# A written order on every engine, q transposed by DMA and merged products in an attention and long-convolution kernel

## The chip, the cores and the metric

The kernel runs on one core of a Trainium2 chip. A core has TensorE (PE in the profile; it loads weights, PEld, and multiplies into PSUM), VectorE (DVE), ScalarE (ACT), GpSimd (POOL) and SyncE (SP), each with its own queue of instructions, and 16 DMA engines that all queues share. SBUF and PSUM have 128 partitions. The metric is the device time of one execution in microseconds (us).

## The reference

Linear attention with an RMS norm feeds a gated long convolution. B = 8 batches, H = 8 heads, S = 576 times, D = 64; d_model is 512.

```python
kv = np.einsum('bhsd,bhse->bhde', k, v)
out = np.einsum('bhsd,bhde->bhse', q, kv)
rms = np.sqrt(np.mean(out * out, axis=-1, keepdims=True) + 1e-06)
x = (out / rms * g_norm)            # then heads side by side: (B, S, 512)

proj = x @ w_proj                   # 512 -> 1536
x1, x2, x3 = proj[..., :D], proj[..., D:2*D], proj[..., 2*D:]   # D = 512 here
X2 = np.fft.rfft(x2, n=S, axis=1)
H = np.fft.rfft(filter_fft, n=S, axis=0)[None, :, :]
x2_conv = np.fft.irfft(X2 * H, n=S, axis=1)
y = (x1 * x2_conv * x3) @ w_out
```

Inputs and output are float32 in DRAM; the kernel computes in bfloat16 with float32 sums.

## The kernel before

**Tiling.** One batch after the other, features on the partitions (four blocks of 128 features, two heads each) until the Fourier stage, frequencies on the partitions there. The Fourier transforms are matmuls with cosine and sine tables (IV, FW, FX), made once at the start (L167 to L210). Symmetries cut them down: time is split into thirds and halves, the sums and differences of these (fold, L291) are what is projected.

**The steps of one batch.** kv (L214) multiplies k and v over time, in four chunks of 128 times and a tail of 64, and evicts the two halves of each head pair into kvblk, a block-diagonal matrix of 128 x 128 per pair. qtr (L236) transposes q with 36 matmuls against an identity and evicts them to qT. att_o (L258) multiplies qT by kvblk, two full matmuls for a feature block, and evicts twice: the square (ACT) and the value times g_norm. att_r (L273) sums the squares of a head by a matmul with the 0/1 matrix ind and evicts the inverse root; att_x multiplies. fold forms rr (192 columns) and ab (384 columns). proj2 (L363) projects both for x2: full blocks of 128 rows, and 64-row rests in matmuls of 64 columns each (L372, L384). fft (L388) has three parts: g = 1 (L404 to L406), g = 0 (L399 to L401), g = 2 (L414 to L416). Each result in PSUM is multiplied twice on DVE with the filter's spectrum HH (L408, L409); the two products are added on POOL (L411) or, for g = 0 of later batches, on DVE (L412). proj13 (L419) makes x1 and x3 (the gates) in 16 matmuls per feature block and multiplies them. inv (L436) is the inverse transform: odd and even parts, one copied by ACT, sum and difference on DVE, three operations of a recombination w, and fin, the product with the gates, giving yg. outp (L484) multiplies yg by w_out in chunks of 128 rows, two chunks per PSUM tile, and stores 64 rows by 2 per DMA on SP's queue; the last 64 rows of two batches share one tile (L492).

**What sets the order.** The text is a loop over batches in which batch b's Fourier and gate steps are interleaved with batch b + 1's attention. The framework's scheduler orders instructions within that; only some are pinned with keep_in_program_order. PSUM is one pool of four tiles of two banks, given out in turn. Loads go through POOL's queue, two batches ahead, k and v each in a main and a tail DMA, q in two halves (L66 to L82); row stores through SP's queue. At the start, 33 matmuls on constant data (warm, L531) are placed on PE between the first steps. The filter is loaded twice, straight and reversed through an indirect DMA (L142, L147), and folded on DVE (L319); gen_h (L332) makes its spectrum.

Of the kernel before, what the change touches and what calls it, by code (L numbers as in the profile page):

```python
# [9 lines left out]
FP32 = mybir.dt.float32  # L10
# [5 lines left out]
P = 128  # L16
MAGIC = 3.0 * (2.0 ** 22)


@with_exitstack  # L20
def kernel(
# [11 lines left out]

# [8 lines left out]
    NSC = 5  # L46
    TAIL = S - 4 * P
    N1 = 97
    NM = 64

    nc.scalar.preload_act_table_set("trig_and_small")
    consts = ctx.enter_context(tc.tile_pool(name="consts", bufs=1))
    work = ctx.enter_context(tc.tile_pool(name="work", bufs=1))
    psp = ctx.enter_context(tc.tile_pool(name="psp", bufs=4, space=bass.MemoryType.PSUM))

    def ps_tile(name):
        return psp.tile([P, 2, 512], FP32, name=name, tag="ps")

    NR = S // 64
    kvm = [[consts.tile([P, H, 4, D], BF16, name="%sm%d" % (n, i)) for n in "kv"] for i in range(2)]
    kvt = [[consts.tile([P, H, D], BF16, name="%st%d" % (n, i)) for n in "kv"] for i in range(2)]
    qb = [consts.tile([P, 4, NR * D], BF16, name="qb%d" % i) for i in range(2)]

    def load_kv(b, *parts):
        for h0, h1 in parts:
            for i, src in enumerate((k, v)):
                nc.gpsimd.dma_start(  # L70
                    out=kvm[b % 2][i][:, h0:h1].rearrange("p h c d -> p h (c d)"),
                    in_=bass.AP(tensor=src.tensor, offset=src.offset + (b * H + h0) * S * D,
                                ap=[[4 * D, P], [S * D, h1 - h0], [1, 4 * D]]))
                if h0 == 0:
                    nc.gpsimd.dma_start(out=kvt[b % 2][i][:TAIL], in_=src[b, :, 4 * P:S, :].transpose([1, 0, 2]))

    def load_q(b):
        for g in range(2):
            nc.gpsimd.dma_start(  # L79
                out=qb[b % 2][64 * g:64 * g + 64].rearrange("p h (m x) -> p (h m) x", m=3),  # L80
                in_=bass.AP(tensor=q.tensor, offset=q.offset + (b * H + 4 * g) * S * D,
                            ap=[[3 * D, 64], [SB * D, 12], [1, 3 * D]]))  # L82


    kvblk = [consts.tile([P, 4, P], BF16, name="kvblk%d" % i) for i in range(2)]
    for i in range(2):
        for t in kvt[i]:
            nc.vector.memset(t[TAIL:P], 0.0)
        nc.vector.memset(kvblk[i], 0.0)
    bias_eps = consts.tile([P, 1], FP32)  # L90
    nc.vector.memset(bias_eps, 1e-6)

    W0 = math.pi / S
    cosb = consts.tile([P, 4], FP32)
    nc.vector.memset(cosb[:, 0:2], math.pi / 2)
    nc.vector.memset(cosb[64:P, 1:2], -math.pi / 2)
    nc.vector.memset(cosb[:, 2:4], -W0)
    nc.vector.memset(cosb[64:P, 3:4], W0)

    ind = consts.tile([P, P], BF16)  # L100
    nc.vector.memset(ind, 0.0)
    for h in range(2):
        nc.vector.memset(ind[64 * h:64 * h + 64, 64 * h:64 * h + 64], 1.0)  # L103

    load_q(0)

    kcol = consts.tile([P, 3], FP32)  # L110
    ki = consts.tile([P, 3], I32)
    nc.gpsimd.iota(ki[:, 0:1], pattern=[[0, 1]], base=0, channel_multiplier=3)
    nc.gpsimd.iota(ki[0:96, 1:2], pattern=[[0, 1]], base=1, channel_multiplier=3)
    nc.gpsimd.iota(ki[96:128, 1:2], pattern=[[0, 1]], base=2, channel_multiplier=3)
    nc.gpsimd.iota(ki[0:64, 2:3], pattern=[[0, 1]], base=2 + 3 * 32, channel_multiplier=3)
    nc.gpsimd.iota(ki[64:128, 2:3], pattern=[[0, 1]], base=2 + 3 * 32, channel_multiplier=3)
    tvi = work.tile([P, 2 * SB], I32, name="tvi", tag="yg", bufs=3)


    nc.gpsimd.iota(tvi, pattern=[[2 * SB, 2], [2, 3], [6, 64]], base=1, channel_multiplier=0)  # L120
    ident = consts.tile([P, P], BF16)
    make_identity(nc, ident)

    load_kv(0, (0, 4), (4, 8))
# [7 lines left out]
    for part in (1, 0, 2):  # L132
        load_w(wp[:, :, part * DM:(part + 1) * DM], moe_w_proj[:, part * DM:(part + 1) * DM])


    fa = work.tile([P, 3, DM], FP32, name="fa", tag="tpw", bufs=2)
    fc = work.tile([P, 3, DM], FP32, name="fc", tag="tpw", bufs=2)
    fidx = consts.tile([P, 3], I32)
    for a, r0, n, base in ((0, 0, 64, 0), (0, 64, 64, 1), (1, 0, 64, 2), (1, 64, 64, SB), (2, 0, 32, SB + 1)):
        nc.gpsimd.iota(fidx[r0:r0 + n, a:a + 1], pattern=[[0, 1]], base=S - 1 - base, channel_multiplier=-3)  # L140
    for r0, n, a, na, base, step in ((0, 64, 0, 2, 0, 2), (64, 64, 0, 2, 1, SB - 1), (0, 32, 2, 1, SB + 1, 1)):
        nc.gpsimd.dma_start(out=fa[r0:r0 + n, a:a + na], in_=bass.AP(  # L142
            tensor=moe_filter_fft.tensor, offset=moe_filter_fft.offset + base * DM,
            ap=[[3 * DM, n], [step * DM, na], [1, DM]]))
    for a in range(3):
        n = P if a < 2 else 32
        nc.gpsimd.indirect_dma_start(out=fc[:n, a], out_offset=None, in_=moe_filter_fft,  # L147
                                     in_offset=bass.IndirectOffsetOnAxis(ap=fidx[:n, a:a + 1], axis=0))

    load_q(1)  # L150
    load_kv(1, (0, 8))
    load_w(wo, moe_w_out)


# [489 lines left out]
```

## Time and profile before

| | |
|---|---|
| runs of the kernel | 240.43, 241.04, 243.11 us; median 241.04 |
| span of the profiled execution (first to last instruction) | 238.0 us |
| PE busy | 213.9 us, 90% |
| DVE busy | 197.2 us, 83% |
| ACT busy | 156.0 us, 66% |
| POOL busy | 72.1 us, 30% |
| mean granted TensorE clock | 0.993 |
| HBM read, written | 33.69 MB, 9.44 MB |

Busy shares are averages over a head that fills the pipeline, a middle of equal rounds and a tail that drains it, so they are to be read stage by stage. Matmul lengths include a pipeline delay and overlap; the distance from one start to the next is what a matmul costs. Idle time of an engine has the engine named that released it.

### The profile page before, as it was taken

The numbers are of one execution on the slowest core, as the hardware profiler recorded it, in microseconds if no ns is written. First come the engines' busy times: TensorE is split into PE (matmuls) and PEld (weight loads), VectorE is DVE, ScalarE is ACT, GpSimd is POOL, SyncE is SP. The second block draws the span as 40 slices with busy tenths as digits, with TensorE's granted clock in tenths as the row PEclk, the third lists the DMA queues.
The fourth block names the chain that finished last, engine by engine and source line by source line (L and its number), as shares of the span: only waits on it lengthen the run. The fifth ranks groups of instructions, "written<-read, shape, count | busy, mean of one in ns | idle before, by whom it ended". The sixth has DMA issues, their size and how long they took to land.

```text
span 238.0 us, 4900 instructions
## 1 busy us (share of the span) xinstructions
PE 213.9 (90%) x1960; PEld 128.5 (54%) x1960; DVE 197.2 (83%) x376; ACT 156.0 (66%) x237; POOL 72.1 (30%) x96
## 2 busy tenths in 40 slices
PE   4978897685999999999999999999999999999960
PEld 1434354363576657665667566656675666566420
DVE  7759574799989798979797989797979897999860
ACT  2754528971887689776977697769776977642520
POOL 7963971490280029000910091002100210021010
PEclk9999999999999999999999999999999999999997
DMA  6999999999099129914992399250033003400346
GB/s 63 163 190 230 227 192 197 191 192 108 3 155 198 45 77 158 203 38 126 121 193 74 91 118 188 83 135 0 4 88 88 3 0 91 132 0 3 94 122 181
DMA packets 45559, 27.17 MB, mean 114 GB/s; under 512 B 22274, under 2 KB 40706, under 8 KB 45538
## 3 DMA queue, kind: packets, MB, share of 16 engines
q0 software_dynamic: 40256, 17.70, 58.8%
q1 hardware_dynamic: 5122, 8.92, 13.9%
q8 instruction: 15, 0.25, 0.4%
q10 hardware_dynamic: 160, 0.26, 0.4%
q14 instruction: 6, 0.05, 0.1%
HBM read 33.69 MB, written 9.44 MB: 181 GB/s over the span
## 4 chain that ended last, share of the span: by engine, by line
PE 61%; ACT 15%; DVE 8%; DMA 8%; issue 3%; POOL 3%; POOLq 0%; DVEq 0%; ACTq 0%
PE ps_x L428 20%; PE ps_out L488 10%; ACT qT L256 6%; PE ps_x L378 6%; DMA fc<-in_moe_filter_fft_dram,fidx 5%; DMA km<-in_k_dram 3%; PE ps_x L384 2%; PE ps_x L369 2%; PE ps_o L265 2%; PE ps_r L280 2%; ACT kvblk L234 2%; PE ps_invo L454 2%; PE ps_inve L454 2%; PE ps_kv L223 2%; ACT osb L271 2%
## 5 line engine op out<-in xcount | busy, mean ns | idle before, releaser
L428 PE MATMUL ps_x<-x,wp 128*128 128x288 bf16 x512 | 68.0, 286 | 1.5 <-DVE FX L210 1.5
L428 PEld LDWEIGHTS <-wp 128*128 128x128 bf16 x512 | 49.8, 98 | 15.3 <-issue 2.6
L411 POOL TENSOR_TENSOR Y<-tpw 128x1024 bf16<-128x1024 f32 (+1 forms) x9 | 21.2, 2354 | 68.7 <-PE ps_x L428 43.2
L434 DVE TENSOR_TENSOR g<-ps_x,x 128x576 bf16<-128x576 f32 x32 | 24.1, 754 | 9.8 <-ACT x L432 9.7
L432 ACT CAST x<-ps_x 128x576 bf16<-128x576 f32 x32 | 20.7, 646 | 10.4 <-PE ps_x L428 10.4
L70 POOL DMA_DIRECT2D km<-in_k_dram x9 | 7.8, 871 | 64.4 <-PE ps_kv L223 64.4
L488 PE MATMUL ps_out<-wo,yg 128*128 128x512 bf16 x112 | 26.6, 379 | 0.0
L281 ACT ACTIVATE rstd<-ps_r,bias_eps 128x576 bf16<-128x576 f32 x32 | 23.3, 742 | 4.8 <-PE ps_r L280 4.8
L496 ACT COPY ot<-ps_out 128x1024 f32<-128x1024 f32 (+1 forms) x17 | 15.9, 937 | 13.8 <-PE ps_out L488 13.8
L266 ACT ACTIVATE sq<-ps_o 128x576 bf16<-128x576 f32 x32 | 20.7, 653 | 5.6 <-PE ps_o L265 5.6
L408 DVE TENSOR_TENSOR tpw<-ps_X,HH 128x1024 f32<-128x1024 f32 (+1 forms) x16 | 19.5, 1221 | 5.1 <-PE ps_X L406 4.4
L271 ACT ACTIVATE osb<-ps_o,g_col 128x576 bf16<-128x576 f32 x28 | 20.8, 742 | 0.0
L409 DVE TENSOR_TENSOR tpw<-ps_X,HH 128x1024 f32<-128x1024 f32 (+1 forms) x16 | 19.4, 1213 | 0.0
L458 ACT COPY os<-ps_invo 128x576 f32<-128x576 f32 x14 | 9.0, 640 | 12.9 <-PE ps_x L372 5.1
L488 PEld LDWEIGHTS <-yg 128*128 128x128 bf16 x112 | 10.8, 98 | 10.4
L265 PE MATMUL ps_o<-qT,kvblk 128*128 128x288 bf16 x64 | 12.8, 287 | 3.7 <-ACT kvblk L234 2.1
L378 PE MATMUL ps_x<-wp,ab 128*128 128x512 bf16 x64 | 15.5, 381 | 0.6 <-DVE ab L307 0.3
L256 ACT COPY qT<-ps_qT 128x1152 bf16<-128x1152 bf16 x14 | 15.1, 1122 | 0.1
L280 PE MATMUL ps_r<-sq,ind 128*128 128x288 bf16 x64 | 13.1, 286 | 1.6 <-ACT osb L271 0.8
L79 POOL DMA_DIRECT2D qb<-in_q_dram x16 | 12.5, 784 | 6.3 <-DMA wp<-in_moe_w_proj_dram 3.1
L535 PE MATMUL ps_w<-kvblk,ind 128*128 128x512 bf16 x33 | 11.1, 486 | 3.7 <-DVE ind L103 3.4
L374 ACT CAST x<-ps_x 128x1024 bf16<-128x1024 f32 x8 | 8.1, 1016 | 8.4 <-PE ps_x L372 8.4
(177 smaller groups left out, 414.8 us busy)
## 6 DMA issues: line engine op xcount, KB each, us to landing
out_dram<-ot SPq DMA_DIRECT2D x28, 256.0 KB, 3.3
qb<-in_q_dram POOLq DMA_DIRECT2D x16, 288.0 KB, 7.1
km<-in_k_dram POOLq DMA_DIRECT2D x7, 512.0 KB, 6.2
vm<-in_v_dram POOLq DMA_DIRECT2D x7, 512.0 KB, 8.4
wp<-in_moe_w_proj_dram POOLq DMA_DIRECT2D x3, 512.0 KB, 10.6
out_dram<-ot SPq DMA_DIRECT2D x10, 128.0 KB, 3.2
km<-in_k_dram POOLq DMA_DIRECT2D x2, 256.0 KB, 5.6
kt<-in_k_dram POOLq DMA_DIRECT2D x8, 64.0 KB, 5.7
```

Source lines behind the costliest of these rows:

```text
L256: nc.scalar.copy(out=o_, in_=i_)
L266: nc.scalar.activation(out=s['sq'][:, j].rearrange("p (a b) -> p a b", a=2), in_=op[:, :, 0:TH], func=AF.Square)
L271: nc.scalar.activation(out=o_, in_=op[:, :, 0:TH], func=AF.Copy, scale=g_col)
L281: nc.scalar.activation(out=s['rstd'][:, j].rearrange("p (a b) -> p a b", a=2), in_=r2[:, :, 0:TH], func=AF.Abs_reciprocal_sqrt, scale=1.0 ...
L378: nc.tensor.matmul(pp[:, h], ab[:, j, h * SB:h * SB + P], wp[:, j, DM:2 * DM], start=(j == 0), stop=(j == NDC - 1))
L408: nc.vector.tensor_mul(out=t_[:n, 0], in0=xp[:n], in1=HH[:n, g, 1:3])
L409: nc.vector.tensor_mul(out=t_[:n, 1], in0=xp[:n], in1=HH[:n, g, 0:2])
L411: nc.gpsimd.tensor_add(out=Y[:n, 2 * g:2 * g + 2], in0=t_[:n, :, 0], in1=t_[:n, :, 1])
L428: nc.tensor.matmul(pp[:, h, 0:TH], w_, x[:, j, h * TH:(h + 1) * TH], start=(j == 0), stop=(j == NDC - 1))
L432: nc.scalar.copy(out=x1, in_=pp[:, :, 0:TH])
L434: nc.vector.tensor_mul(out=st[b]['g13'][:, dc].rearrange("p (a b) -> p a b", a=2), in0=pp[:, :, 0:TH], in1=x1)
L488: nc.tensor.matmul(pp[:, cc], yg[:, dc, c * P:(c + 1) * P], wo[:, dc], start=(dc == 0), stop=(dc == NDC - 1))
```

## The change

The file is rewritten; the mathematics stays. What it does:

- **Order.** The framework's scheduling is switched off (manual_schedule). The steps have names, and three strings list them: FIRST for the start up to the first rounds, ROUND for each batch, LAST for the end. A plus is one batch ahead, a minus one behind. Each engine runs its instructions in the order in which the strings issue them. A step in ROUND that was done already, or that a batch does not have, is skipped. PSUM tiles are taken and freed by name, the one freed longest ago first. The three batches of the start are interleaved differently; the steps that would issue warm-up matmuls (W0_ and so on) are in no string, so there are none.
- **k, v, q** are loaded with six consecutive times per partition, 96 partitions, one DMA each per batch; kv runs over six chunks of 96. Time has another order inside the batch, which the evictions by_time undo.
- **q.** For batches 2 to 7 one DMA transpose on SP's queue (Qt) replaces the matmuls and evictions; a copy of two elements on POOL, queued behind it, waits for it. Batches 0 and 1 keep 24 matmul transposes each.
- **att_o.** kvblk is no longer block-diagonal: four matmuls of 64 x 64 instead of two of 128 x 128.
- **128-column rests.** abT, F1, F2 and the shared last output rows use full matmuls of 128 columns, with tables padded by zeros (FY, FZ).
- **Merged tables and products.** The tables' angles are made in one pass; the two products of fft are one instruction of 2048 columns; fold, w and fin run over four feature blocks at once. The sum for g = 0 is on POOL, for g = 1 on DVE, in all batches.
- **Filter.** Loaded once in bfloat16; straight plus and minus reversed is formed by matmuls (Ff), not by a second load.
- **Output.** Chunks begin at 64 rows' offset in odd batches; rows go out as four DMAs of 32 rows by 2 per pair of chunks. The last batch has its own chunks (V), and half of its inverse transform sums odd and even parts on PE (J).

```diff
+ROUND = """eab+ eT+ u23 Gb2 O01++ F1+ sq0++ sq1++ g2 rrM+ ob0++ ob1++ w rrT+ err+ K+++ U2- M1+ R3++ eK+++ ot2- F0+ rs3++
+Ga1+ Ga0+ x11+ fin Lq++++ R1++ x10+ M0+ Gb0+ F2+ R2++ rs1++ g0+ Gb1+ R0++ rs2++ M2+ Ga3+ A0+ g1+ Lv++++ rs0++
+Av1+ x1++ Lk++++ x13+ O23+++ sq3+++ Gb3+ U0 g3+ sq2+++ ob3+++ I01+ Io01+ ob2+++ x0++ U4 ot0 fd++ os01+ fa++
+Ga2+ ot4 Io23+ x12+ Qt++++ abM++ u01+ I23+ fr++ os23+ abT++"""
...
+FIRST = """Zd Zi Z Lq Zt Lkb An T0 Zf eTv0 Lvb Tb0 Tb2 Lva Lka T1 Act Lf Kb eKb eTv1 Lq+ Tb1 O23 Ka sq2 sq3 R3 Lw1 eKa
+ov3 O01 ov2 rs3 sq1 sq0 ov1 R2 ov0 rs2 Ff2 Ff1 x1 Ff0 fd1 fr1 R0 Lw3 T0+ rs0 Lv+ R1 rs1 eTa0+ x0 H2 H0 fd0 H1
+Ga0 Ga1 HN0 Gb0 x11 Gb1 Lk+ fr0 Lw2 x10 Lq++ g0 Ga2 T1+ x12 g1 K+ eTa1+ Lv++ Gb2 fa1 eK+ O01+ rrM HN1 fa0 sq1+
...
+    ctx.enter_context(tc.manual_schedule())
...
+    def Qt(b):
+        nc.sync.dma_start_transpose(out=qT(b), in_=kvq["q"][b % 2].rearrange("p h c d -> p (h c d)"))
+        nc.gpsimd.tensor_copy(out=one_, in_=qT(b)[0:1, 0, 0:2])
...
+    def O(b, j):
+        op = tmp['o', b, j] = take(("o", b, j))
+        for r in range(2):
+            for hp in range(2):
+                nc.tensor.matmul(op[64 * hp:64 * hp + 64, r, 0:TH], kvblk[b % 2][64 * r:64 * r + 64, r ^ hp, j],
+                                 qT(b)[64 * r:64 * r + 64, 6 * j + 3 * hp:6 * j + 3 * hp + 3].rearrange("p c (m t) -> p m c t", m=3),
+                                 start=True, stop=True)
...
-                nc.tensor.matmul(pp[64 * h:64 * h + 64, 0], ab[:, j, h * SB + P:(h + 1) * SB], wp[:, j, DM:2 * DM],
-                                 start=(j == 0), stop=(j == NDC - 1))
+            nc.tensor.matmul(pp, abt()[:, j, P:2 * P], w2(j), start=(j == 0), stop=(j == NDC - 1))
...
+        for ri in range(2):
+            mm(xp[:, ri], FY if ri else FW[:, 0, 2], x2[:, 2 + ri], start=True, stop=False)
+            mm(xp[:, ri], FZ[:, ri], x2[:, 4], start=False, stop=True)
...
-            nc.vector.tensor_mul(out=t_[:n, 0], in0=xp[:n], in1=HH[:n, g, 1:3])
-            nc.vector.tensor_mul(out=t_[:n, 1], in0=xp[:n], in1=HH[:n, g, 0:2])
+        two = bass.AP(tensor=h.tensor, offset=h.offset, ap=[list(h.ap[0]), [DM, 2], [DM, 2], [1, DM]])
+        vec.tensor_mul(out=t_[:n], in0=xp[:n].unsqueeze(1).to_broadcast([n, 2, 2, DM]), in1=two)
...
+    def U_ev(b, c0):
+        ot = ot_tile(b)
+        act.copy(out=ot, in_=tmp['u', b, c0])
+        free(("u", b, c0))
+        for i in range(4):
+            nc.sync.dma_start(out=o_rows(b, 2 * (b % 2) + 4 * c0 + i, 2 * (b % 2) + 4 * c0 + 4 + i), in_=ot[32 * i:32 * i + 32])
```

The names in the strings: L load, K kv matmuls, eK its eviction, T and eT q transposes by matmul (eT without a or v: eviction of abT), O, sq, ob or ov the attention and its evictions, R and rs the norm, x its product, fd, fr, fa the fold, rr and ab the projections with evictions err and eab, F the Fourier matmuls, M the products, A and Av the sums, Ga and Gb the gate matmuls with x1 and g their evictions, Io and I the inverse with os and u, w, fin, U and ot the output and its stores, Tb tables, H and HN the filter's spectrum.

More of the change, by code (lines that the diff above doesn't have):

```diff
@@ L56, in ps_tile @@
[L56 to L75, printed above, removed]
@@ L90 @@
[L90 to L105, printed above, removed]
```

964 lines of the change are left out of this document (544 added, 420 removed).

## The prediction

> **What bounds the kernel now.** I read the totals first, then busy time by stretch (cut where a batch's first projection of x2 begins), then one batch on TensorE in order of time, then the costs of the operations that the change merges or removes, and last the head and the tail.
>
> The page's first part and the stretches; the columns are the stretch, its length, busy time (instructions) of PE, PEld, DVE, ACT and POOL, the granted clock, DMA share and GB/s:
>
> ```profile
> span 238.0 us, 4900 instructions
> ```
> ```profile
> 0.00:10.00 10.00, 6.60 (x32) 2.46 (x34) 7.47 (x35) 4.42 (x11) 8.54 (x21) 1.00 0.98 108
> 10.00:20.00 10.00, 8.12 (x98) 4.27 (x93) 6.65 (x15) 6.95 (x13) 7.00 (x14) 1.00 1.29 185
> 20.00:30.00 10.00, 8.02 (x58) 3.82 (x58) 7.02 (x17) 3.86 (x6) 6.48 (x15) 1.00 1.28 231
> 30.00:40.00 10.00, 8.80 (x82) 4.77 (x81) 6.61 (x10) 4.67 (x8) 4.86 (x9) 1.00 1.48 196
> ...
> 50.00:59.00 9.00, 5.42 (x50) 3.79 (x48) 9.00 (x20) 3.28 (x6) 3.87 (x4) 1.00 1.28 146
> ...
> 131.00:156.00 25.00, 24.73 (x241) 15.45 (x241) 22.13 (x40) 19.12 (x28) 6.96 (x7) 1.00 0.80 119
> 156.00:179.60 23.60, 23.37 (x232) 15.14 (x231) 20.69 (x38) 18.52 (x27) 2.35 (x1) 1.00 0.20 53
> 179.60:204.50 24.90, 24.65 (x240) 15.48 (x240) 22.05 (x40) 19.12 (x28) 2.36 (x1) 1.00 0.19 47
> ```
>
> Three stages. From 59.0 to 204.5 six rounds (one batch each) take 145.5 us, 24.25 each, and PE is busy 99% of each: the middle is TensorE's, with DVE second at 21.4 us a round (22.13 and 20.69, averaged). In the head, up to 59, PE is the idle one: in its last 9 us DVE is busy 9.00 and PE 5.42. The tail is 33.5 us. So a term of the sum counts in the middle only if it takes PE time away; in the head it counts if work that PE can do comes forward.
>
> One round on PE (start, length, operation):
>
> ```profile
> 132.53 1.90 PE L378 MATMUL ps_x<-wp,ab 128*128 128x512 bf16 x8
> 134.36 1.05 PE L384 MATMUL ps_x<-wp,ab 128*64 128x512 bf16 x8
> 135.25 0.29 PE L223 MATMUL ps_kv<-vm,km 128*64 128x64 bf16 x8
> ...
> 135.88 1.18 PE L247 MATMUL ps_qT<-ident,qb 128*64 128x128 bf16 x36
> 136.98 0.61 PE L404 MATMUL ps_X<-x,FW 128*128 128x512 bf16 x2
> 137.52 0.39 PE L405 MATMUL ps_X<-x,FW 64*128 64x512 bf16 x1
> 137.53 0.39 PE L406 MATMUL ps_X<-x,FX 64*128 64x512 bf16 x1
> 138.03 0.41 PE L265 MATMUL ps_o<-qT,kvblk 128*128 128x288 bf16 x2
> 138.28 2.12 PE L428 MATMUL ps_x<-x,wp 128*128 128x288 bf16 x16
> 140.24 0.41 PE L280 MATMUL ps_r<-sq,ind 128*128 128x288 bf16 x2
> ```
>
> The lengths overlap, so I price by start to start: a full 512-column matmul takes 0.22 us (eight in 132.53 to 134.36), sixteen gate matmuls 1.96, two matmuls on disjoint halves of the array the time of one (137.52 and 137.53).
>
> **The change, part by part.** The sum is made against the span of 238.0 us; the median of the runs, 241.04, lies 3.0 above it, and I add that at the end.
>
> *PE in the six middle rounds.* (a) The 36 transposes of q go to a DMA for batches 2 to 7: 135.88 to 136.98, 1.10 us a round. (b) F1 becomes four full matmuls, 0.88 for 1.05 (136.98 to 138.03): 0.17. (c) The ab tail becomes four full matmuls, 0.88 for 0.89 (134.36 to 135.25): nothing; the same exchange in F2 (three full for two full and a pair) and in the shared last output rows (four full for eight of 64 columns) I take at nothing too. (d) k and v come in six chunks of 96 rows instead of five, 48 matmuls for 40: 0.63 (135.25 to 135.88) becomes 0.76, 0.13 lost. (e) att_o turns two full matmuls (0.25) into four on the quarters of the array. The nearest rows are the pair on two halves that started together (137.52, 137.53), so four together could take 0.13; if only two overlap it is 0.25, if none 0.50: from 0.5 gained to 1.0 lost a round. Leaving and entering the split array also costs: F1's one pair at 137.5 stretched 0.66 of matmuls to 1.05, about 0.2 for each of the two changes of shape. After the change att_o runs as two calls of two groups, so 2 x (2 x 0.13 + 2 x 0.2) = 1.3 for the 1.0 of now, or at 0.1 per change 0.9. I take zero. The Trainium skill says the same against this edit: "Mode switching requires drain" (TensorEngine Tiling, Tiling Modes, Key Properties); by that alone the four extra switches would make O slower by about 0.3 a round, 2 us in all. The trace agrees that there is such a cost (the 1.05).
>
> Together 1.10 + 0.17 - 0.13 = 1.14 a round, 24.25 to 23.1, and **6.8 us over six rounds**.
>
> *Does DVE or ACT become the bound?*
>
> ```profile
> L470 DVE TENSOR_TENSOR yg<-w,g 128x1152 bf16<-128x1152 bf16 x14 | 10.6, 754 | 0.3
> ...
> L470 DVE TENSOR_TENSOR yg<-w,g 128x576 bf16<-128x576 bf16 x4 | 1.8, 456 | 0.1
> ```
>
> Two of the small take 912 ns, one of twice the size 754, so an instruction merged away saves about 0.16 us. Per batch 13 go (two products, seven of the fold, three of w, one fin): 2.1, DVE 21.4 to 19.3. ACT loses the two q evictions, 2.14 in the chain of waits below, and gains a third small kv eviction: 19.1 to under 17.5. Both stay under 23.1. These are cover, not gain.
>
> *The q transposes.*
>
> ```profile
> 136.87 2.14 ACT qT L256 x2
> ```
>
> These two evictions stand on the chain in every round; they and the transposes go, and PE, busy 99%, remains the limit there. In their place SP issues them, behind the row stores and behind the arrival of q; POOL then waits, in its tiny copy, until the transposed q has landed, and the next loads and one product sum (2.35 us of POOL) queue behind that.
>
> ```profile
> out_dram<-ot SPq DMA_DIRECT2D x28, 256.0 KB, 3.3
> qb<-in_q_dram POOLq DMA_DIRECT2D x16, 288.0 KB, 7.1
> ```
>
> No row shows such a DMA. It moves 576 KB within the chip: 3.3 us if it lands like one store, 14.2 if like two q loads in turn; I take 7.5, the store scaled by bytes. It is issued about two thirds of a round ahead of its first reader, 15 us, so it costs nothing up to that. A load costs POOL 0.8 us (six loads and the sum make the 6.96 of 131 to 156) and lands in 7.1, so the circle (q load, transpose, copy, next q load) takes 7.9 + T and fits into 23.1 up to T = 15.2.
>
> *The head.* The q, k, v loads of a batch are 0.58 MB each in SBUF, the projection weights 1.5, the filter now 0.6 once. Up to the third weight part the new order loads q0, k0, v0, filter, q1, two weight parts, v1, k1, third part: 5.6 MB; the stretches above moved 1.08, 1.85, 2.31, 1.96 MB, so 5.6 arrives at about 32 us, k1 at 30.
>
> ```profile
> L408 DVE TENSOR_TENSOR tpw<-ps_X,HH 128x1024 f32<-128x1024 f32 x8 | 9.8, 1221 | 4.4 <-PE ps_X L406 4.4
> ...
> L374 ACT CAST x<-ps_x 128x1024 bf16<-128x1024 f32 x8 | 8.1, 1016 | 8.4 <-PE ps_x L372 8.4
> ```
> ```profile
> 3.40 6.16 PE L535 MATMUL ps_w<-kvblk,ind 128*128 128x512 bf16 x14 [3.40 <-DVE ind L103]
> ...
> 10.61 2.12 PE L535 MATMUL ps_w<-kvblk,ind 128*128 128x512 bf16 x9
> ...
> 21.17 0.76 DVE L289 TENSOR_TENSOR x<-osb,rstd 128x1152 bf16<-128x1152 bf16 x1
> ```
>
> x of batch 0 is complete at 21.9 now. The new order hangs on the same loads and puts two of the filter's evictions (1.02 each on ACT) between: about 23.9, H before the gates, first gate at 25.5. Then along the written order on PE, with the prices above: five gate halves (0.98 each) to 30.4, q1's second transposes, k1's products 32.0 to 32.8 (its load), a gate half 33.8, half of O 34.3, rr 1.4 and ab 1.8 to 38 (the third weight part at 32 is there), F0 0.66 to 38.6, ab tail, O and F1 to 40.9. From here DVE is the later: the product on F0 takes 2 x 1.22 to 41.0, that on F1 to 43.5, F2's 44.7, a sum 45.9, x of batch 1 (0.76 twice) 47.4, a gate 0.75, the first part of the fold about 1.5: batch 1's projection starts near 50, while PE fills in gates and batch 2's products. It starts at 59 now; at that point the new order has also done a gate half, K, half of O and one R of later batches (2.2 us), less one inverse half. That is 11 us ahead if nothing waits. The warm-up matmuls are gone, and they show the price: fourteen took 6.16 us, 0.44 each, nine later ones 2.12, 0.24 each, at a granted clock of 1.00 in both rows. If the filter and H matmuls (27 slots of 0.22, 5.9 us) run at the slow pace, up to 5.9 is lost. I take 2.5 off for this and for waits: **9 us gained**, between 0 and 11.
>
> *The tail.*
>
> ```profile
> 229.20 1.76 PE ps_out L510 x7
> 230.98 0.69 DVE ot__3338 L516
> ```
>
> For half of the last batch the inverse is summed on PE, twice the matmuls: twelve more of 192 and 96 columns for two blocks, 1920 columns, 0.8 at 0.22 per 512. After the last matmul there is one eviction and a store now, 7 us; afterwards eviction, a second eviction behind two DMA issues on ACT, four issues on POOL, a landing: 7 again. F1 gives 0.2 back. **0.6 lost**, 2 either way.
>
> Sum: 238.0 - 6.8 - 9 + 0.6 = 222.8, and 3.0 beside the span: 225.8, **226 us**.
>
> **The rivals.**
> *The transposes go block by block.* 24 blocks of 96 x 128 in turn; at 1 us each T = 24, the circle is 31.9, 8.8 over the round, six times: 226 + 53 = 279, slower. It decides from T = 15.2, and from 15.2 + 15.2 / 6 = 17.7 the whole gain is gone. For it: a store of 256 KB lands in 3.3, so landing is mostly a fixed time, and paid 24 times it is far over; against it: it is one DMA, and the other DMAs of the page have their pieces in flight together. The Trainium skill speaks for it: a 128 x 128 bf16 block takes 390 ns on TensorE and 1309 by the DMA crossbar (VectorE: DVE Perf Modes, The three transpose paths); by an estimate from that page 24 in turn would be 31 us. No row of this trace tests it. Chance 0.07.
> *The written order waits.* Every engine now keeps one order; a late eviction holds all that follows. DVE at 19.3 of 23.1 and four PSUM pairs leave little slack. If the rounds keep their 24.25: 232.6; if the head gains nothing either: 241.6. For it: DVE and PE already wait for each other at 50 to 59. Against: between the kernel's F and inverse steps the new round puts some 10 us of gates and outputs. Chance 0.20 for 233 to 243.4, and 0.02 for more.
> *The head stays slow-clocked.* Ff, H and then the first gates at half pace: 5.9 more than the forecast's 2.5 allows for, about 229 (5.9 - 2.5 on top). The Trainium skill has the rule (TensorE: Matmul & The Clock Gate, The HAM clock gate): slow until some 3.4 us of sustained work. The first fourteen matmuls agree. It lies within the forecast's range.
> *Better.* Four quarters at once without cost (0.5, seven times: 3.5), a head with no wait (2), and the 1% of idle gone from six rounds (1.5): 226 - 7 = 219. Chance 0.14 for under 221.
>
> **How the numbers follow.** Forecast (221 to 233) 0.57, better 0.14, order waits 0.22, transposes 0.07. About 1%, 2.4 us, is what a measurement tells from no change. Faster by more than that is under 238.6: 0.57 + 0.14 + 0.13 of the waiting order = 0.84; within 1%: 0.07; slower: 0.07 + 0.02 = 0.09. The range: 6.8 may be 3 to 11, the head 0 to 11, the tail 2 either way; leaving out 2 in 10, 216 to 238.
>
> **What would show it.** Rounds of 23.1 with PE at 98% and no q transposes; O near 0.25 a call; the first gate at 25 and batch 1's projection at about 50; transposes landing under 15 us, and no POOL copy idle that delays a load; DVE under 20 a round. It is wrong if a round shows PE idle over 1 us behind DVE or ACT, if POOL's copy waits past the next q load, or if the gates of batch 0 start after 30.

## The result and the profile after

| | kernel before | changed kernel |
|---|---|---|
| runs beside each other | 240.43, 241.04, 243.06, 243.11 us; median 242.05 | 222.67, 222.83, 224.6, 227.95 us; median 223.72 |
| ratio | | 0.922, 95% interval 0.915 to 0.929 |
| span of the profiled execution | 238.0 us | 226.2 us |
| batch 1's projection starts | 59.0 (two of its matmuls at 57.2, the rest from 58.7) | 54.5 |
| six rounds up to batch 7's projection | 145.5 us | 140.1 us |
| from there to the end | 33.5 us | 31.5 us |

The forecast was 226.0 us (216 to 238). The profiled execution of the changed kernel is the longest of its four, 227.95 us for a span of 226.2, and it is left out of the ratio as a slow one; one wait that it shows, below, accounts for about 4.7 us.

The first part of its page, to be held against the 238.0 us, 213.9 us of PE and 197.2 us of DVE of before:

```profile
span 226.2 us, 4505 instructions
## 1 busy us (share of the span) xinstructions
PE 203.2 (90%) x1809; PEld 124.6 (55%) x1809; DVE 186.0 (82%) x276; ACT 149.9 (66%) x232; POOL 48.8 (22%) x61
```

PE and DVE lost about 11 us each, and the span 11.8. Shares of busy time have hardly moved: the work has shrunk on the bound.

Busy time by stretch, with the columns of before; the last four rows are the rounds of batches 3 to 6, cut where a projection of x2 begins:

```profile
10.00:20.00 10.00, 9.40 (x107) 5.94 (x108) 5.62 (x15) 7.92 (x16) 4.02 (x6) 1.00 1.23 207
20.00:30.00 10.00, 9.98 (x75) 3.64 (x73) 7.32 (x13) 6.08 (x8) 0.58 (x1) 1.00 1.29 205
30.00:40.00 10.00, 10.00 (x127) 6.78 (x125) 8.16 (x17) 6.39 (x12) 0.00 (x0) 1.00 1.30 204
...
106.74:128.78 22.04, 22.01 (x207) 14.10 (x206) 20.38 (x25) 16.95 (x28) 4.04 (x4) 1.00 0.75 135
128.78:151.60 22.82, 22.82 (x211) 14.41 (x210) 20.76 (x27) 17.37 (x28) 4.89 (x5) 1.00 0.83 157
151.60:173.55 21.95, 21.95 (x207) 14.02 (x206) 20.56 (x26) 16.96 (x27) 2.54 (x2) 1.00 0.28 62
173.55:194.66 21.11, 21.11 (x147) 13.36 (x146) 20.04 (x25) 13.14 (x19) 2.35 (x1) 1.00 0.25 63
```

Two things are to be seen. The rounds are 22.0 and 22.8 us instead of 23.8 and 24.9, and PE has no idle time left in them; the round of batch 6 is shorter still, since nothing of a later batch has to be prepared in it. And from 10 to 40 us, where PE was 83% busy before, it is 98% busy: the head now waits for PE, and no longer for loads, up to 40 us.

What PE does in a round, from start to start, summed from the rows of one round of each kernel (155.78 to 179.55 us before, 151.60 to 173.55 us after), in us; kinds of work that differ by 0.03 and less are left out:

| | before | after | taken in the prediction |
|---|---|---|---|
| transposes of q | 1.11 | 0 | -1.10 |
| F1 | 1.04 | 0.88 | -0.17 |
| O (four feature blocks) | 0.97 | 0.75 | 0 (-0.5 to +1.0) |
| PE idle between R and F0 | 0.28 | 0 | not in the sum |
| K (key-value products) | 0.63 | 0.86 | +0.13 |
| gates | 7.84 | 8.03 | not in the sum |
| outputs | 3.55 | 3.45 | not in the sum |
| ab, its full matmuls | 1.83 | 1.73 | not in the sum |
| rr, its 64-column rest | 0.55 | 0.46 | not in the sum |
| inverse, its 97-row matmuls | 0.48 | 0.36 | not in the sum |
| whole round | 23.77 | 21.95 | -1.14 |

In the rounds that hold the shared output rows, these went from 0.98 to 0.86.

Some of these rows only trade time with their neighbours, since a change of the array's shape lengthens the matmul ahead of it, too. The 0.19 that the gates gained stands ahead of the two calls of O, and about 0.1 of K's 0.86 is its way back to full matmuls, which the rest of rr had to pay before. The part on the prediction shows both.

The head on PE, as start, length and operation:

```profile
12.28 1.17 PE L375 MATMUL ps<-ident,qb 96*128 96x96 bf16 x12
...
19.48 0.61 PE L281 MATMUL ps<-fn,ident 96*32 96x512 bf16 x1
...
24.11 0.42 PE L419 MATMUL ps<-sq,ind 128*128 128x288 bf16 x2
24.36 0.68 PE L375 MATMUL ps<-ident,qb 96*128 96x96 bf16 x12
...
25.30 1.84 PE L301 MATMUL ps<-ff,FW 128*64 128x512 bf16 x12
27.07 3.60 PE L298 MATMUL ps<-ff,FW 128*97 128x512 bf16 x12
30.60 3.60 PE L575 MATMUL ps<-x,wp 128*128 128x288 bf16 x28
```

The same twelve transposes of q take 1.17 us at 12.28 and 0.68 at 24.36: the pace of PE doubles in between, at about 23.4 us. The filter's 36 matmuls fill 19.48 to 24.11, 4.63 us. The 24 matmuls of H follow, 25.30 to 30.60, and the first gate starts at 30.60 (27.44 in the kernel before).

The chain of waits between 63 and 89 us, and GpSimd's own rows there:

```profile
63.29 9.73 DMA qT<-qb
...
73.14 0.18 POOL one__100 L367
...
73.62 10.81 DMA vb<-in_v_dram
...
84.56 1.30 PE ps L341 x48
85.86 3.05 PE ps L698 x8
```
```profile
73.14 0.18 POOL L367 COPY one__100<-qT 1x2 bf16<-1x2 bf16 x1 [6.34 <-DMA qT<-qb]
73.62 0.80 POOL L107 DMA_DIRECT2D vb<-in_v_dram  x1 [0.31 <-issue]
```

GpSimd's two-element copy waited 6.34 us for a transposed q, and v of batch 4 was issued only behind it. Its products on PE, at 84.56, waited 3.4 us for that load, and the eight output matmuls behind took 3.05 us for the usual 1.73. The mean granted clock from 84 to 90 us is 0.72. These are the 4.7 us.

The DMA issues of the page, with the median time to landing, which was 7.1 us for a half-size q load before:

```profile
qb<-in_q_dram POOLq DMA_DIRECT2D x8, 576.0 KB, 12.9
...
qT<-qb SPq DMA_TRANSPOSE x6, 6.7
```

### The profile page after: what moved, and what is told of

Read it like the earlier page. It is cut to its first block, busy times and chain, and to the rows that moved or that the text cites. A ratio compares the mean times of both kernels' runs of the same rounds, so it can differ in the third digit from the quotient of the medians.

```text
span 226.2 us, 4505 instructions
## 1 busy us (share of the span) xinstructions
PE 203.2 (90%) x1809; PEld 124.6 (55%) x1809; DVE 186.0 (82%) x276; ACT 149.9 (66%) x232; POOL 48.8 (22%) x61
## 4 chain that ended last, share of the span: by engine, by line
PE 77%; DMA 9%; DVE 6%; ACT 3%; issue 2%; ACTq 1%; POOL 1%; POOLq 0%
PE ps L575 25%; PE ps L698 11%; PE ps L502 5%; DMA vb<-in_v_dram 5%; DMA qT<-qb 4%; PE ps L602 3%; PE ps L419 3%; PE ps L488 3%; PE ps L508 3%; PE ps L341 3%; PE ps L412 2%; PE ps L281 2%; PE ps L542 2%; PE ps L495 2%; PE ps L737 2%
## 5 line engine op out<-in xcount | busy, mean ns | idle before, releaser
L575 PE MATMUL ps<-x,wp 128*128 128x288 bf16 x512 | 70.6, 286 | 0.5 <-DVE g L583 0.5
L550 DVE TENSOR_TENSOR tpw<-ps,HH 97x2048 f32<-97x2048 f32 (+1 forms) x16 | 36.6, 2286 | 10.1 <-PE ps L527 9.9
L556 POOL TENSOR_TENSOR Y<-tpw 97x1024 bf16<-97x1024 f32 x8 | 18.9, 2357 | 94.4 <-DVE tpw L550 94.4
L581 ACT CAST x<-ps 128x576 bf16<-128x576 f32 x32 | 20.4, 642 | 13.9 <-PE ps L575 10.3
L583 DVE TENSOR_TENSOR g<-ps,x 128x576 bf16<-128x576 f32 x32 | 23.9, 753 | 5.9 <-PE ps L575 4.8
L433 ACT ACTIVATE rstd<-ps,bias_eps 128x576 bf16<-128x576 f32 x32 | 23.4, 745 | 7.8 <-PE ps L419 7.6
L698 PE MATMUL ps<-wo,yg 128*128 128x512 bf16 x112 | 27.7, 392 | 0.0
L512 ACT CAST x<-ps 128x1024 bf16<-128x1024 f32 (+1 forms) x24 | 20.8, 873 | 7.9 <-PE ps L502 3.1
L422 ACT ACTIVATE sq<-ps 128x576 bf16<-128x576 f32 x32 | 19.5, 654 | 4.0 <-PE ps L412 4.0
L429 ACT ACTIVATE o<-ps,g_col 128x576 bf16<-128x576 f32 x28 | 19.7, 755 | 0.0
```

What stands on the lines that cost most here:

```text
L422: act.activation(out=halves(sq()[:, j]), in_=tmp['o', b, j][:, :, 0:TH], func=AF.Square)
L429: act.activation(out=by_time(osb(), j), in_=i_, func=AF.Copy, scale=g_col)
L433: act.activation(out=by_time(rstd(), j), in_=by_row(tmp['r', b, j]), func=AF.Abs_reciprocal_sqrt, scale=1.0 / D, bias=bias_eps)
L512: act.copy(out=o_(), in_=tmp[key, b])
L550: vec.tensor_mul(out=t_[:n], in0=xp[:n].unsqueeze(1).to_broadcast([n, 2, 2, DM]), in1=two)
L575: nc.tensor.matmul(pp[:, h, 0:TH], w_, x[:, j, h * TH:(h + 1) * TH], start=(j == 0), stop=(j == NDC - 1))
```

## The experiments

Each run has its ratio to the kernel before on its own chip, with the 95% interval.

**The changed kernel again**, unchanged.

> The changed kernel as it is, for a second profile and for the comparison with the three that follow. If the stand of TensorE at 81 to 84.6 us (the v load of batch 4 behind the copy that waits for a transpose) belongs to the written order, it is there again, 2 to 4 us long, at 222 to 228 us. If it was an accident of one execution, the rounds run through without it and the time is under 222.

223.92 us (222.84 to 229.56), ratio 0.9315 (0.926 to 0.937). The profiled execution, its longest, has no wait for v at all; it has a longer slow pace:

```profile
29.83 6.29 PE L298 MATMUL ps<-ff,FW 128*97 128x512 bf16 x12
36.05 6.29 PE L575 MATMUL ps<-x,wp 128*128 128x288 bf16 x40
```

The twelve matmuls that took 3.60 us above take 6.29, and the first gate starts at 36.05. So the two long executions seen are long for different reasons, and the slow pace in the head ends at a moment that differs between executions.

**The v load moved ahead of the copy** (in the opening's written order):

```
-... g1+ F1+ g0+ ... Lv++++ x10++ ...
+... Lq++++ Lv++++ sq2++ ...
```

> In the start list the v load of batch 4 stands right behind the q load of batch 4, ahead of the copy that waits for batch 3's transpose; nothing else is moved. Theory (the load is late only because POOL's queue stands): the stop of 3.4 us at 81 and the slow matmuls behind it (8 in 3.05 instead of 1.73) go, 4 to 5 us against the profiled 226.2 us span, 2 to 4 against the median of the changed kernel. Rival (the DMA engines are full there, share 1.15): v lands as late as before, since it shares the engines with the q and k loads, and less than 1 us is gained.

225.38 us (224.54 to 226.02), ratio 0.9389 (0.934 to 0.944).

```profile
77.30 0.44 PE L412 MATMUL ps<-qT,kvblk 64*64 64x288 bf16 x8 [1.65 <-DMA qT<-qb]
```

The wait for v is gone, and a wait of 1.65 us for a transposed q stands in its place. The chain of waits has that transpose at 13.15 us where it had 9.73; that the v load beside it takes DMA time from it is the likely reason, and wasn't tested by itself. Its head is also 1.1 us longer in the profile (batch 1's projection starts at 55.68). Nothing was gained.

**GpSimd's copy left out**, so that loads do not queue behind the landing of a transpose:

```
-        nc.gpsimd.tensor_copy(out=one_, in_=qT(b)[0:1, 0, 0:2])
```

> The copy on POOL behind each q transpose is left out, so POOL's loads no longer wait for transposes anywhere. Theory (POOL's stand is the cost): as much as with the early v load, 2 to 4 us against the changed kernel, and no other round changes, since they have PE at 99 to 100% already. Rival (the copy keeps loads away from running transposes, and without it transposes land later than their readers): landing of the transposes rises from 6.7 us to over 12, PE waits at O, and the time is the same or up to 5 us longer.

224.4 us (222.69 to 225.61), ratio 0.9345 (0.927 to 0.942). The load of v goes out at 66.96 instead of 73.62, and no wait of PE between 40 and 110 us is left that is worth a line:

```profile
66.96 0.80 POOL L107 DMA_DIRECT2D vb<-in_v_dram  x1
...
82.21 1.53 POOL L107 DMA_DIRECT2D qb<-in_q_dram  x2 [13.68 <-DMA qT<-qb]
```

Still the time of the unchanged kernel, within intervals of 1.4 and 1.8 us either way. The wait itself goes with the copy: of five profiles with the copy in its place and v loaded behind it, four show PE waiting for v, 0.97 to 3.9 us in all (the second profile of the changed kernel has none), and none of those without the copy does. What it costs the median is too small to be seen here.

**Fourteen filler matmuls ahead of the first transposes** (`W0_ W1_` before `T0` in the opening; 10 and 4).

> Fourteen warm-up matmuls are put back ahead of the first transposes of q. Theory (the slow clock costs in the head, where PE is busy 94 to 100% from 10 to 40 us): the filter matmuls of 19.5 to 24.1 take 2.2 us instead of 4.6, the tables and K about half, the first gate comes at 27 to 28 instead of 30.6, and 2 to 3.5 us are gained. Rival (the loads or DVE and ACT set the head): the first gate moves forward but what follows waits for k1 or the third weight part, and the gain is under 1 us.

224.8 us (223.23 to 229.0), ratio 0.9345 (0.929 to 0.940). The first twelve transposes take 0.68 us instead of 1.14, but after 1.40 us of idle time PE is slow again by 11 us (the six table matmuls at 11.28 take 0.82, as without fillers) and stays so to 24, and the first gate starts at 30.98. Fillers at the very start buy nothing.

```profile
10.00:20.00 10.00, 9.29 (x107) 5.83 (x108) 5.68 (x15) 7.96 (x16) 3.48 (x5) 0.53 1.23 207
```

This is the stretch from 10 to 20 us, to be held against that of the changed kernel above: the lengths of the matmuls are the same half-pace ones in both, but the granted clock reads 0.53 here and 1.00 there. So in these two profiles the column shows a fall from full pace, and not that full pace has not been reached yet.

**Fillers spread over the first 20 us**, 14 ahead of the first transposes, 6 in the gap ahead of the tables, 2 at five later places (the counts are set in one more line):

```
-Zd Zi Z Lq Zt Lkb An T0 Zf eTv0 Lvb Tb0 Tb2 Lva Lka T1 Act Lf Kb eKb eTv1 Lq+ Tb1 O23 Ka
+Zd Zi Z Lq Zt Lkb An W0_ T0 Zf eTv0 Lvb W1_ Tb0 Tb2 Lva Lka W2_ T1 Act Lf W3_ Kb eKb eTv1 Lq+ W4_ Tb1 W5_ O23 W6_ Ka
```

> The changed kernel with filler matmuls put among the first 20 us of TensorE's work: 14 ahead of batch 0's first transposes, 6 in the 1.4 us gap ahead of the table transposes, and 2 at each of five later places, as the kernel before had 14, 9, 2, 3, 2, 3. Theory A (the head of the changed kernel lost its time because matmuls ran at half pace from 10 to 24 us, and to about 38 us in an unlucky execution, for want of dense work): matmuls run at full pace from about 10 us on; the 36 filter matmuls take about 2.5 us instead of 4.6, the first gate starts at 27 to 28 instead of 30.6, and the time falls by 2 to 3 us to 220 to 222 with no execution above 225. Rival B (the pace there does not hang on filler work, or the head waits for ScalarE's and VectorE's evictions and loads anyway): the fillers cost their own 10 x 0.21 = 2.1 us or are hidden, the first gate stays at 30 to 32, and the time is 223 to 226.

224.0 us (221.99 to 227.1), ratio 0.9283 (0.924 to 0.933). The profiled execution, 221.99 us, shows the mechanism: full pace from 10 us, 36 filter matmuls in 2.7 us, first gate at 28.27, batch 1's projection at 52.21 instead of 54.5. The median shows no gain. Why other executions of it reach 226 and 227 us isn't seen in this one profile; the next run speaks for the copy.

**Spread fillers, and the copy left out.**

> The same fillers, and GpSimd's two-element copy behind each DMA transpose left out as well, so that the loads queued behind it go out at once. If the slow pace of the head and the wait for v of batch 4 (3.4 us) are two separate losses, both gains add: 217 to 220 us, no TensorE wait above 1 us between 40 and 110 us. If the gain of either is taken up again by the next thing that is late (as moving the v load gained nothing), it equals the run with fillers alone to within 1 us.

221.4 us (221.24 to 221.82), ratio 0.9211 (0.918 to 0.924), on the chip on which the fillers alone gave 224.0. This is the fastest version, and its six executions lie within 0.6 us:

```profile
18.71 0.41 PE L418 MATMUL ps<-sq,ind 128*128 128x288 bf16 x2 [0.41 <-DVE o L426]
19.05 0.39 PE L281 MATMUL ps<-fn,ident 96*32 96x512 bf16 x1
...
24.76 3.60 PE L298 MATMUL ps<-ff,FW 128*97 128x512 bf16 x11
28.28 3.97 PE L574 MATMUL ps<-x,wp 128*128 128x288 bf16 x31
```

Each of the two edits alone left the time where it was, as far as the intervals tell (0.9315 unchanged, 0.9345 and 0.9283 alone, each 0.005 to 0.008 either way); together they take 2.5 us. That two gains, each too small to be seen alone, simply add up isn't excluded by this. The likely reading, from the profiled executions, is that with the copy in place PE's earlier start meets late loads (it still waits 1.0 us for v with the fillers alone), and at slow pace early loads meet a late PE.

**Only the first 20 of these fillers, and no copy.**

> As the run with fillers and without GpSimd's copy (221.4 us), but only the 14 fillers ahead of batch 0's transposes and the 6 in the gap ahead of the table transposes; the ten later ones (10 x 0.21 us of TensorE) are gone. Theory A (the gap of 1.4 us alone lets the pace fall): full pace still holds from 10 us on, the first gate starts 1 to 2 us earlier than in that run, and the time is 219 to 221. Rival B (the small matmuls from 12 to 19 us do not hold the pace by themselves): the filter matmuls take over 4 us again, first gate at 29 to 31, and 222 to 225 us.

223.0 us (221.8 to 223.66), ratio 0.9259 (0.923 to 0.929). Rival B came true:

```profile
16.45 0.64 PE L418 MATMUL ps<-sq,ind 128*128 128x288 bf16 x2 [0.67 <-ACT sq L421]
...
18.60 0.61 PE L281 MATMUL ps<-fn,ident 96*32 96x512 bf16 x1
```

The pair of R matmuls takes 0.64 here and 0.41 with the later fillers. The pace holds through the transposes and products from 10 to 15 us, then three idle pieces of 0.4 to 0.7 us come within 3 us, and it falls (granted clock 0.80 from 10 to 20 us, 0.65 from 20 to 24); the first gate starts at 29.86.

**The DMA transpose left out altogether**, with the copy; batches 2 to 7 read the transposed q of batches 0 and 1.

> The changed kernel with the DMA transpose and the copy behind it left out for batches 2 to 7: those batches read the transposed q of batches 0 and 1, so their output is that of other q. Theory A (beside the hold on GpSimd's queue the DMA transposes cost nothing, since 4.7 to 11 us of landing fit a round): the same time as the run without the copy, 222 to 225 us, and loads of q, k and v land no earlier. Rival B (they slow the loads and evict work from the DMA engines in the head): 1.5 to 4 us less, 219 to 222, and q's load lands in about 7 us instead of 13.

223.69 us (222.67 to 225.2), ratio 0.9308 (0.927 to 0.935): the time of the unchanged kernel. q's load still lands in 13.1 us (median), so it isn't the transposes that slow it. As placed here, they cost nothing that can be measured. They do come late at times: PE waits 0.4 and 1.1 us for a transposed q in the two profiles with fillers and no copy, in the opening.

**q transposed on PE again**, all else as changed (`Qu` stands behind `Qt` in the strings):

```
-        nc.sync.dma_start_transpose(out=qT(b), in_=...)
-        nc.gpsimd.tensor_copy(out=one_, in_=...)
+        q_mm(b, 0)
+        q_ev(b, 0, act.copy)
+    @one
+    def Qu(b):
+        q_mm(b, 1)
+        q_ev(b, 1, act.copy)
```

> The changed kernel with q of batches 2 to 7 transposed by TensorE again (24 matmuls of 96x128 and two ScalarE evictions a batch) in place of the DMA transpose and the copy behind it; all else unchanged. Theory A (rounds are bound by TensorE): at 0.68 us for 12 of them at full pace a batch costs 1.36 us more of TensorE, so 6 x 1.36 = 8.2 us more, less the 3.4 us of the wait for v of batch 4 that goes with the copy: 228 to 232 us, rounds of 23.2 to 23.5 us instead of 22.0. Rival B (the written order and the merged work gave the gain, and TensorE has slack to take the transposes): 222 to 225 us, rounds at 22.0 to 22.3.

239.63 us (238.43 to 240.4), ratio 0.996 (0.992 to 1.000): worse than both theories said. PE waited for the evictions of the transposes, 4.7 us in all in its profile, and batch 2's projection starts at 92.4 us instead of 79.6.

**The same, with the two halves apart** in the rounds, at places where PSUM buffers are free.

> As the run with matmul transposes, but with the two halves of a batch's transposes taken apart and set where one of four PSUM buffers is held, so that no matmul behind them waits for ScalarE's 1.12 us eviction (batch 4 on; batches 2 and 3 are transposed in the written opening as in that run; the load of q of batch 6 goes out with its round instead of in the opening). That run had rounds of 23.7 to 24.7 us, 1.02 us more of TensorE work and 0.85 us of waiting for evictions. Theory A (the DMA transpose is worth its TensorE time, the rest was the place of the transposes): rounds of 23.0 us, and 230 to 236 us, 4 to 9 us below that run. Rival B (ScalarE's two evictions a batch delay the round wherever they stand): rounds stay at 23.7 us and the time at 237 to 240.

236.93 us (235.82 to 237.4), ratio 0.9839 (0.981 to 0.987); nearer to rival B. Two of its rounds, and a row of PE in the second:

```profile
87.05:111.09 24.04, 23.07 (x227) 14.81 (x226) 20.30 (x25) 18.66 (x29) 3.16 (x2) 1.00 0.39 80
111.09:135.05 23.96, 23.08 (x231) 15.28 (x230) 20.35 (x26) 18.89 (x29) 4.63 (x4) 1.00 0.67 119
```
```profile
122.79 0.68 PE L380 MATMUL ps<-ident,qb 96*128 96x96 bf16 x12
124.67 1.14 PE L580 MATMUL ps<-x,wp 128*128 128x288 bf16 x8 [0.84 <-ACT qT L384]
```

In the second, that of batch 3, PE is busy 23.08 us, 1.07 over the 22.01 of the same round of the changed kernel, and idle 0.88: the gates wait for ScalarE's eviction of the transposes, which holds a PSUM buffer. That is 1.9 us a round, and more in the opening, where batch 2's projection starts at 87.05 instead of 79.57. Other places might cost less; they weren't tried.

**The kernel before, without its transposes of q** for batches 2 to 7, which read that of batch 1:

```
+        if b >= 2:
+            s['qTc'], s['qT'] = st[b - 1]['qTc'], st[b - 1]['qT']
+            return
```

> The kernel before with the 36 TensorE transposes of q and their two ScalarE evictions left out for batches 2 to 7, which read the transposed q of batch 1, so their output is that of other q. Theory A (the rounds before are bound by TensorE, the transposes are worth 1.10 us each): 6 x 1.10 = 6.6 us less, 233 to 235 us, rounds of 23.1 us. Rival B (the planner's order has other waits that fill the space): 237 to 240. Rival C (ScalarE's evictions, 2 x 1.1 us a batch, were on the path too): 228 to 232.

232.42 us (231.75 to 233.53), ratio 0.9663 (0.963 to 0.969); 8.0 us less than the kernel before beside it, 1.34 a batch, between A's 6.6 and C.

```profile
150.90:173.27 22.37, 22.37 (x199) 14.17 (x196) 20.86 (x38) 16.53 (x25) 2.37 (x1) 1.00 0.22 58
```
```profile
155.78:179.55 23.77, 23.54 (x234) 15.20 (x232) 20.86 (x38) 18.52 (x27) 2.35 (x1) 1.00 0.21 54
```

The first fence is this run, the second the same kind of round of the kernel before (to be held against 150.90 to 173.27). PE's busy time fell by 1.17, and the 0.23 us of idle that the round had are gone too. The chain of waits of the kernel before shows where they were, in the round from 155.78:

```profile
161.62 2.14 ACT qT L256 x2
...
164.94 0.54 ACT x L432
...
165.52 0.38 PE ps_X L399
```

F0 on PE (165.52) waited for ScalarE's eviction of a gate half (164.94), which stood behind 2.14 us of transposed q. With those two gone, this round of the run has no such wait.

**The merged products split again**, two of 1024 columns for one of 2048:

```
-    vec.tensor_mul(out=t_[:n], in0=xp[:n]...to_broadcast([n, 2, 2, DM]), in1=two)
+    for i in range(2):
+        vec.tensor_mul(out=t_[:n, i], in0=xp[:n], in1=...)
```

> The changed kernel with each merged product of 2048 columns (2.28 us on VectorE, two a batch) made as two of 1024 columns again (1.22 and 1.21 us in the kernel before), so VectorE has 2 x 0.15 us more a batch. Theory A (VectorE at 20.4 of a round's 22.0 us is cover): no difference that can be measured, 222.5 to 225 us, rounds at 22.0. Rival B (VectorE's chain from the products to the inverse matmuls is as tight as TensorE): 0.3 us or more a round, 225.5 to 228 us.

224.39 us (222.75 to 225.73), ratio 0.9321 (0.928 to 0.936), that of the unchanged kernel run again (0.9315). A round as above, of batch 5:

```profile
148.12:170.07 21.95, 21.95 (x207) 14.02 (x206) 20.70 (x28) 16.94 (x27) 2.52 (x2) 1.00 0.30 65
```

DVE works 0.14 us more in it and the round is the same 21.95, as are those of batches 4 and 6 (22.8 and 21.1). Two earlier rounds are 0.7 and 0.8 us longer than in the run without the copy, with waits for v in them (0.47 and 0.74 us), not for DVE. VectorE is cover.

## Why the prediction was right, and where it was not

The total was off by 2.3 us, 1% of the measurement, with larger errors of both signs inside; that it came so close is partly luck. With the 4.7 us of the one wait taken out, the six rounds gave 10.1 us for 6.8, the head 4.5 for 9, the tail gained 2.0 instead of losing 0.6, and the time beside the span was 1.75 (227.95 less 226.2) for the 3.0 that was added. 238.0 - 10.1 - 4.5 - 2.0 + 1.75 is 223.1 us. (Executions of the kernel before that have their span on record lie 1.7 to 2.2 us above it; the 3.0 also held the distance of a quick profiled execution from the median.)

**The rounds** are bound by PE, as said; removal of the transposes from the kernel before shortened them at once. The sum was too small: 1.14 a round were taken, and the rounds of batches 3 to 5 are 1.7 to 2.0 us shorter. (That of batch 6 is 3.7 shorter, since its work for later batches is done ahead.) Two terms were under-sized.

The transposes were priced at their 1.10 us on PE; the run without them gave 1.34, because about 0.24 of idle time behind their evictions went as well. The prediction saw these two evictions on the chain in every round and still called them cover; the 1% of idle it put under "better".

The rests, but for F1, were taken at nothing and gave some 0.2. A change of the array's shape lengthens the last matmul ahead of it by 0.09 us. Eight full ab matmuls took 1.83 from start to start ahead of 64-column ones (132.53 to 134.36 in the prediction's rows), and take 1.73 ahead of full ones:

```profile
168.06 1.89 PE L502 MATMUL ps<-wp,ab 128*128 128x512 bf16 x8
169.78 0.33 PE L602 MATMUL ps<-IV,Y 128*128 128x192 bf16 x2
```

The eight output matmuls that stood ahead of F2 show the same, 1.82 before against 1.73. The rests themselves changed little: the ab tail from 0.89 to 0.86, F2 from 0.67 to 0.65, the shared rows by 0.12 every second round. F1 at 0.17 (measured 0.16) was right, and so was K at 0.13: the other 0.1 of its 0.23 is the change back to full matmuls, which the rest of rr no longer pays (0.55 to 0.46). Why the inverse's 97-row matmuls take 0.12 less was not looked into.

On O, taken at nothing between 0.5 gained and 1.0 lost, the prediction set a row against a rule: the Trainium skill says that a change of tiling mode needs a drain (TensorEngine Tiling, Tiling Modes, Key Properties). The trace agrees, and has the price. Eight matmuls on quarters of the array, between full ones:

```profile
116.78 1.14 PE L575 MATMUL ps<-x,wp 128*128 128x288 bf16 x8
117.86 0.44 PE L412 MATMUL ps<-qT,kvblk 64*64 64x288 bf16 x8
118.23 1.15 PE L575 MATMUL ps<-x,wp 128*128 128x288 bf16 x8
119.22 1.89 PE L698 MATMUL ps<-wo,yg 128*128 128x512 bf16 x8
```

The eight gate matmuls ahead take 1.08 us from start to start, those behind 0.99: entering the quarters costs 0.09, and it is found in the gates. The call itself takes 0.37, with the way back in it. Together that is 0.46 for two blocks, which cost 0.49 before as two pairs of full matmuls. So the overlap of four quarters just outweighs the two changes of shape, and O gained some 0.04 a round, not the 0.22 of its own row. It is the 0.9 that the prediction worked out for 0.1 per change, and nothing was the right term.

**VectorE and ScalarE as cover**: right for VectorE, though its 2.1 us were over-sized. DVE is at 20.4 to 20.8 in rounds of 22 (19.3 was predicted, from 21.4), and 0.14 more changed nothing. ScalarE was not quite cover in the kernel before: its two evictions of q are the 0.24 above.

**The DMA transposes**: T was taken as 7.5 us; six landed in 4.7 to 11.1 us, median 6.7. The rival "block by block", 24 us and more, is refuted: such a transpose of 576 KB lands in about the time of an ordinary transfer. The Trainium skill's 1309 ns for one 128 x 128 block (VectorE: DVE Perf Modes, The three transpose paths) is no price for the blocks of one large transpose: 24 of them in turn would be 31 us by that page, an estimate, and the trace has 6.7. That they cost nothing is shown by the run without them. What the prediction did not price is the copy's hold in the opening, where two transposes and the loads of two batches are in flight together: 6.34 and 10.41 us of POOL, and 3.4 us of PE in this profile. Its own sign for that, a copy idle that delays a load, came true; in the median it can't be seen.

**The head** is the step that failed: 9 us were taken, 4.5 came, and the first gate started at 30.6 instead of 25.5, beyond the bound of 30 that the prediction itself had set. From the first gate to batch 1's projection it took 23.9 us, for the 24.5 of the prediction, so the loss lies ahead of the first gate. The path there was right, and two prices on it were wrong.

The first is the pace. The prediction took the time of x of batch 0 over from the kernel before, where fillers stood among these matmuls, reserved 2.5 us for slow filter and H matmuls, and named slow pace as a rival worth 229 us. PE was 94 to 100% busy from 10 us on, at half pace to 23.4 us, though the rival had full pace come after some 3.4 us of sustained work. x came at 27.3 instead of 23.9 (25.4 with the spread fillers):

```profile
26.56 0.76 DVE L447 TENSOR_TENSOR x<-o,rstd 128x1152 bf16<-128x1152 bf16 x1 [0.72 <-ACT rstd L433]
```

The second is H. The filter's and H's matmuls were priced at 27 slots of 0.22, 5.9 us. At full pace, with the spread fillers, the filter takes 2.7 and H 5.3, 8.0 together. The prediction left 1.6 us between x and the first gate; it was 3.3, filled with H. H takes 5.3 in every profile but the one that was still slow there, and the rows of the kernel before had it, 3.5 and 1.8 from start to start:

```profile
33.04 3.58 PE L342 MATMUL ps_h<-ff,FW 128*128 128x512 bf16 x12
...
38.84 1.84 PE L345 MATMUL ps_h<-ff,FW 128*64 128x512 bf16 x12 [1.10 <-DVE HH L356]
```

Every third of the first twelve works on 32 rows, so that the array changes its shape eight times; at 0.09 each, an estimate from the rows above, that is most of the 0.9 by which 3.5 exceeds twelve times 0.22.

The spread fillers show what the pace alone is worth: they brought the first gate to 28.27 and batch 1's projection to 52.2 us, at about 2.2 us of PE's time for the ten later ones (0.22 each). Whether the 50 of the prediction can be reached by full pace without fillers, no run shows.

**The written order waits**: one such wait, for v of batch 4, took 3.4 us here and 3.9 in the run with fourteen fillers. The four rounds behind show none.

**The tail**: PE's part was priced as twelve matmuls more; the stretch from batch 7's projection to the end became 2.0 us shorter instead. What of this belongs to the last rows going out by chunk and what to work already done ahead of that mark was not separated.

How the whole gain of 16.7 us (240.63 to 223.92, same chip) divides: 8.0 came by taking the transposes out of the kernel before; putting them back into the changed kernel cost 13.0 at best (223.92 to 236.93, on two chips with 240.63 and 240.44 us for the kernel before). A part of the difference is waiting for evictions, 0.88 us a round there. The remaining 3.7 to 8.7 us are the other edits on PE and the order of the opening, which were not taken apart further.

## What to carry to other kernels

Price work that is taken off the bound engine at its busy time plus the idle time that its own evictions cause there; both went here, 1.17 and 0.23 us a round. Charge a change of the array's shape to the matmul ahead of it as well, and look for it in the neighbour's row: O's own row gained 0.22 us, and 0.19 of it came back in the gates. Where a change fills an idle stretch of the head with work, price that work at the pace which the trace shows for such work there, not at the full one, and look at what kept the pace up before: the fillers that looked like waste were part of it. Two edits that each changed nothing clear of noise (223.9 us to 224.4 and 224.0) gave 2.5 us together, so a failed single experiment doesn't acquit its cause.

## What the runs showed of the hardware

- PE's pace can be half while it is 94 to 100% busy with small matmuls (64 to 288 columns, 10 to 19 us here). The granted clock of the stretch reads 1.00 when full pace has not come yet (the changed kernel), and 0.53 when it came and was lost (the run with fourteen fillers). Length of a known operation is the sign to look at: 1.17 or 0.68 us for twelve transposes of 96 x 128.
- Full pace was lost within 3 us in the run with fourteen fillers, between 7.93 (twelve transposes, 0.68 us) and 11, though PE's longest gap there was 1.40 us. The Trainium skill has the pace fall after an idle window of about 3.4 us (TensorE: Matmul & The Clock Gate, The HAM clock gate); here it fell without a gap of that length. The wait of 3.4 us for v agrees with it: half pace behind it (eight output matmuls in 3.05 for 1.73 us, granted clock 0.72), and none behind the wait of 1.65 us. Ten fillers of 512 columns, two at a time among the small matmuls, held full pace.
- The moment at which full pace comes differs between executions of one kernel: 23.4 us and after 36 us in two profiles of the same code.
- Four matmuls on the quarters of the array overlap: eight of 288 columns in 0.37 us. A change of the array's shape costs 0.09 us, on the matmul ahead of it (1.08 for 0.99 us, 1.83 for 1.73).
- A 576 KB transpose within the chip by DMA lands in 4.7 to 11.1 us and, placed two thirds of a round ahead, costs nothing that can be measured.
